# A new list order for every engine, from a planner that prices dependent neighbours on ScalarE and VectorE

## The chip, the cores and the metric

The kernel runs on one core of one Trainium2 chip. The metric is the device time of one execution in microseconds (us). Each run has a state: fast, or slow when it is over 1.5% above the fastest run of the same kernel. Fast runs are compared with fast runs. All inputs are drawn anew from one fixed seed, and every kernel's output is compared with the reference.

## The reference

```python
# x: 8 batches x 8 heads x 512 tokens x 64; state: 8 x 8 x 32 x 64, both fp32
scores = scale * x @ state.T;   a  = softmax(scores);   xread = a  @ state
scores2 = scale * state @ x.T;  a2 = softmax(scores2);  sread = a2 @ x
attn = concatenate([xread, sread], axis=2)          # 544 rows a batch
x = attn.transpose(0, 2, 1, 3).reshape(8 * 544, 512)
h = x @ w_in                                        # w_in  512 x 2048
r = maximum(h, 0)
g = s * (r * r) + b                                 # s, b: scalars
out = g @ w_out                                     # w_out 2048 x 512, fp32 out
```

## The kernel before

The kernel never forms `xread`. For each batch it multiplies the state by `w_in` (blocks `M`, after `Mps`), and a hidden tile `h` is the attention weights `a` times `M`. ScalarE applies the relu, VectorE squares it into `g`. The product with `w_out` (tiles `wo`, four quarters) is plain for batch 0 and uses one Strassen level for the rest, with operand sums `pd` (of `g`) and `u` (of `wo`) made by VectorE. The bias `b` times the column sums of `w_out` (`wsum`) is added at the end, so `wsum` needs all four `wo` quarters.

`E` holds exponentiated scores. `aT` is `E` transposed by a DMA; only `V`, the state's own read, computes with it (and a gate, shown below, holds the load of batch 3's x until batch 1's `aT` has landed). `xT` is the transposed x of batches from 2 on, needed by `T`, their scores. `wo` quarter 3 (`wo3`) is the last weight to arrive.

What runs on the chip is a set of fixed lists, one per engine. They are made when the program is built, by a list scheduler with durations and priorities.

```python
class Plan:
    def order(self, filler, fill_until, ready):
        def settle(i):                  # when may operation i start?
            own = set(ops[i][0])
            since[i] = max(
                [ops[i][8]]             # "after": never planned earlier than this
                + [ready[n] + (0.0 if own == {made_on.get(n)} else self.hop) for n in ops[i][3]]
            )
# ... each free engine takes the ready operation of lowest priority number ...
                end = done = now + dur
                if land is not None:
                    kind, span = land
                    if kind == "load":
                        done = max(channel, end + 2.0) + span     # fixed here, once
                        channel = max(channel, done)
# ...
                    elif kind == "tp" and e == "SP" and now < channel + 4.0:
                        done = end + max(span, min(8.0, 6.0 - 0.75 * (now - channel)))
                        channel = max(channel, now + 2.0) + 1.1
# ...
    SEQ = "wi0 wi1 wi2 wo0 wo1 wi3 wo2 x2 wo3 x1 x0 x3"      # the loads' order on GpSimd's queue
# ... loads: nc.gpsimd.dma_start, fp32 in memory to fp16 on chip
            if b == 3:                                        # x of batch 3 waits for aT of batch 1
                nc.gpsimd.tensor_copy(gate, A[1]["aT"][:, :, 0, 0])
# ... the transposes of E, on SyncE's queue
            nc.sync.dma_start_transpose(a["aT"][:, g], a["E"][g])
            add(
                ("SP", 1.2), kD + 5, aT_dma(b, g), [("E", b, g)] + [("q", b)] * 0,
                [("aT", b, g)], [Eb, ("aT", f"aT{b}")], ("tp", K["la"] if b < 2 else K["lb"]), after=K["a2"] + 2 * g,
            )
# ... at the end the lists are emitted in order of planned time
    for step in sorted(plan.order(filler, 14.0, landed), key=lambda t: t[:2]):
        step[3](step[2])
```

`channel` is the time until which the planner takes the DMA engines as busy, and `after=K["a2"]` the earliest planned time of the `aT` transposes.

The softmax here doesn't subtract the row's maximum and nothing guards it: scores larger than these inputs give would overflow.

Of the kernel before, what the change touches and what calls it, by code (L numbers as in the profile page):

```python
# [13 lines left out]
class Plan:  # L14


    def __init__(self, caps, hop=0.2, look=0.4, solo=0.0, late=0.0):
        self.caps, self.hop, self.look, self.solo, self.late = caps, hop, look, solo, late
        self.ops, self.pool_of, self.users = [], {}, {}

    def add(self, eng, key, fn, needs=(), makes=(), bufs=(), land=None, tiled=False, after=0.0, spare=0.0):
# [6 lines left out]
    def order(self, filler, fill_until, ready):  # L28
        ready = dict(ready)
        ops = self.ops  # L30
        waits, count, cand = {}, {}, {e: set() for e in ("PE", "ACT", "DVE", "POOL", "SP")}
        since, made_on = {}, {}

        def settle(i):
            own = set(ops[i][0])
            since[i] = max(
                [ops[i][8]]
                + [ready[n] + (0.0 if own == {made_on.get(n)} else self.hop) for n in ops[i][3]]
            )
            for e in ops[i][0]:  # L40
                cand[e].add(i)

        for i, o in enumerate(ops):
            open_ = [n for n in set(o[3]) if n not in ready]
            count[i] = len(open_)
            for n in open_:
                waits.setdefault(n, []).append(i)
            if not open_:
                settle(i)
# [25 lines left out]
        while done_n < len(ops) and now < getattr(self, "horizon", 1e9):  # L75
            for e in free_at:
# [9 lines left out]
                look = self.look if e in ("ACT", "DVE") else 0.06  # L86
# [26 lines left out]
                i = best[1]  # L113
# [28 lines left out]
                for m in makes:  # L142
                    for j in waits.pop(m, ()):
                        count[j] -= 1
                        if count[j] == 0:
                            settle(j)
# [15 lines left out]
def kernel(  # L162
# [17 lines left out]
    B, H, S, D = x.shape  # L180
# [29 lines left out]
    def att_ps(shape, dtype, name):  # L210
        return psA.tile(shape, dtype, tag="att", name=name)

    def mm(out, lhsT, rhs, start=True, stop=True, tp=None, is_transpose=None):
        return nc.tensor.matmul(  # L214
            out,
            lhsT,
            rhs,
            start=start,
            stop=stop,
            tile_position=tp,  # L220
            is_transpose=is_transpose,
            skip_group_check=True,
        )
# [22 lines left out]
    def xf_part(b, i):  # L246
        return xf[2 * b + i // 2][:, 2 * (i % 2) : 2 * (i % 2) + 2]
# [9 lines left out]
    for i in range(4):  # L257
# [15 lines left out]
    ident32 = konst.tile([P, P], FP32, name="ident32")  # L273

    K = dict(
        h1=16.1, hs=1.0, M0=-6.0, M1=4.5, T1=13.8, x2=17.3, T2=21.6, D2=23.7, M2=46.3, V0=38.1, V1=37.9, u=27.3,
        us=-13.3, pd1=13.7, o0=25.7, o2=34.4, w=23.8, r=4.7, T=-9.2, D=10.2, Mb=5.5, V=-3.3, S=3.3, S0=-1.1,
        E=-3.5, L=-5.8, E0=-4.8, L0=0.4, E1=-10.7, L1=-2.6, a4=-9.1, Mc=10.1, pd=19.7, solo=18.2, f0=6.0,
        f1=17.4, mc=-12.4, hsr=-8.2, Ssr=2.8, jE00=17.6, jE01=14.7, jL00=5.7, jL01=21.9, jR00=5.9, jR01=-2.7,
        jE10=2.7, jE11=-4.4, jL10=-8.1, jL11=-22.4, jR10=-2.0, jR11=-2.5, jM0=-1.9, jM1=6.2, xc=1.5, a2=38.2,  # L280
        lx=9.7, la=8.1, lb=11.1, rs=29.4, xs=-1.4, x1=10.8, rL=1.3, a4L=-14.8, McL=5.6, mcL=1.9, soloL=8.6,
    )
    A = {b: {"E": {}, "a4": {}} for b in range(B)}
    G, PD, U, SN, OSB = {}, {}, {}, {}, {}
# [18 lines left out]
    def copy_on(e, dst, src):  # L303
# [11 lines left out]
        solo=K["solo"], late=K["soloL"],  # L315
# [55 lines left out]

    gate = konst.tile([P, 2], FP16, name="gate")
    nc.gpsimd.tensor_copy(gate, xf_part(0, 2)[:, 0, 0:2])
    SEQ = "wi0 wi1 wi2 wo0 wo1 wi3 wo2 x2 wo3 x1 x0 x3"
    seq = [(t[:-1], int(t[-1])) for t in SEQ.split()]
    for n, it in enumerate(seq):
        key = -40 + n
# [40 lines left out]
    for k in range(16):  # L418
        b, i = 4 + k // 4, k % 4
# [108 lines left out]
    def E_exp(b, g):  # L528
        def fn(e):
            a = A[b]  # L530
            if "rs" not in a:
                a["rs"] = apool.tile([P, NG, 2], FP32, name=f"rs_{b}", tag="rs", bufs=3)
            a["E"][g] = apool.tile([P, S], FP16, name=f"E_{b}_{g}", tag=f"E{g}", bufs=4)
            for m in range(2):
                kw = {} if b < 2 else dict(accum_out=a["rs"][:, g, m : m + 1])
                nc.scalar.activation(  # L536
                    a["E"][g][:, 256 * m : 256 * m + 256], a["T"][m][:, g, :], AF.Exp, scale=scale, **kw
                )
# [5 lines left out]
    def E_sum(b, g):  # L544
        def fn(e):
            nc.scalar.activation(junk, A[b]["E"][g], AF.Copy, accum_out=A[b]["rs"][:, g, 0:1])

        return fn

    def D_mm(b, g):  # L550
        def fn(e):
            A[b][f"D{g}"] = att_ps([P, S], FP32, f"D_{b}_{g}")
            mm(A[b][f"D{g}"], bones16, A[b]["E"][g])

# [16 lines left out]
    def a4_mul(b, g):  # L571
        def fn(e):
            A[b]["a4"][g] = apool.tile([P, S], FP16, name=f"a4_{b}_{g}", tag=f"a4{g}")
            ENG[e].tensor_mul(A[b]["a4"][g], A[b]["E"][g], A[b][f"R{g}"])

# [85 lines left out]
    for b in range(B):  # L661
# [71 lines left out]
        for g in range(2):  # L733
            Eb, Rb, a4b = (f"E{g}", f"E{b}{g}"), (f"R{g}", f"R{b}{g}"), (f"a4{g}", f"a4{b}{g}")
            Dps = ("att", f"D{b}{g}")
            rs = ("rs", f"rs{b}")
# [363 lines left out]
    for b in [*range(1, B), "sr"]:  # L1100
        nb = B if b == "sr" else b
        for n in range(7):
            bank, xa, xw, first, last = STEPS[n]
            own = [("att", f"osr{bank}")] if b == "sr" else []
# [70 lines left out]
```

## Time and profile before

| | before |
|---|---|
| median of the first 3 runs | 209.92 us (209.05 to 346.59) |
| profiled run | 209.67 us, fast, clock 1.00 |
| TensorE busy | 97% of the span |
| wait on `wo3` ends (GpSimd) | 33.73 us |
| column sums `wsum` start | 35.14 us |
| `T` of batch 2 starts | 47.45 us |
| first `V` starts | 54.59 us |

The run of 346.59 us is a single outlier and enters no comparison.

The timelines of TensorE, VectorE and GpSimd have four marks. The columns are start (us), duration, engine, source line, operation, out<-in, sizes and count, and in brackets the idle time just before and what ended it:

```profile
35.14 1.05 PE L214 MATMUL wsum_ps<-wo,ones 128*32 128x512 f16 x16
47.45 0.43 PE L214 MATMUL T<-xT,stT 64*32 64x256 f16 x16
54.59 0.42 PE L214 MATMUL V<-xn,aT 128*32 128x64 f16 x32
...
34.28 0.42 DVE L892 TENSOR_TENSOR u<-wo 128x512 f16<-128x512 f16 x1
...
33.73 0.18 POOL L406 CAST stf<-wo 128x2 f32<-128x2 f16 x1 [4.77 <-DMA wo<-in_moe_w_out_dram]
```

The GpSimd line is a small copy that starts as soon as `wo3` has landed, so it is a clock for that transfer. There is no DMA among the four parts of the chain. Two pieces of the chain itself, in order of time (start, duration, what):

```profile
35.82 1.14 DVE g L813 x2
...
49.57 0.61 DVE M L307
```

### The profile page before, as it was taken

How to read it: one execution, taken by the hardware profiler on the slowest of the kernel's cores; microseconds unless marked ns; L12 is line 12 of the kernel's file. 1: busy time of each engine (PE TensorE's matmuls, PEld its weight loads, DVE VectorE, ACT ScalarE, POOL GpSimd, SP SyncE). 2: the span in 40 equal slices, each digit the busy share in tenths (PEclk: the TensorE clock that was granted, in tenths of full speed). 3: DMA queues.
4: the chain of work that ended last, by engine and by line, in shares of the span. 5: the costliest groups of instructions: out<-in, count | busy, mean ns of one | idle time of the engine just before them, and what ended most of it. 6: DMA issues, size and time to landing. Idle time of an engine off the chain costs nothing.

```text
span 207.9 us, 4900 instructions
## 1 busy us (share of the span) xinstructions
PE 201.5 (97%) x1956; PEld 133.5 (64%) x1956; DVE 172.0 (83%) x340; ACT 131.2 (63%) x291; POOL 42.4 (20%) x67
## 2 busy tenths in 40 slices
PE   7998999998999999999999999999999999999993
PEld 3832444444767777666667766776677667888882
DVE  3588997999889686799999999999997999787652
ACT  2489998715675467878865877478756884465000
POOL 0853000132512131411602150411021101200000
PEclk9999999999999999999999999999999999999999
DMA  6999999997998529757972474363013502111132
GB/s 192 303 205 203 206 211 199 143 246 155 162 210 102 140 75 171 123 129 105 145 120 95 110 119 92 79 154 83 0 50 111 102 3 57 54 50 52 52 128 76
DMA packets 44423, 26.05 MB, mean 125 GB/s; under 512 B 26480, under 2 KB 42608, under 8 KB 44400
## 3 DMA queue, kind: packets, MB, share of 16 engines
q0 software_dynamic: 14976, 15.73, 39.8%
q1 hardware_dynamic: 29136, 9.84, 25.9%
q8 instruction: 15, 0.25, 0.5%
q10 hardware_dynamic: 288, 0.16, 0.3%
q14 instruction: 8, 0.07, 0.1%
HBM read 19.43 MB, written 8.91 MB: 136 GB/s over the span
## 4 chain that ended last, share of the span: by engine, by line
PE 86%; DVE 8%; ACT 4%; issue 1%
PE o L214 45%; PE h L214 23%; PE h_sr L214 3%; PE osr L214 3%; PE Mps L214 3%; PE warm_ps L214 3%; PE xTps L214 2%; DVE g L813 2%; PE D L214 2%; ACT g L806 1%; PE V L214 1%; DVE pd L829 1%; DVE osb L966 1%; PE T L214 1%; DVE pd L838 1%; DVE pd L840 1%
## 5 line engine op out<-in xcount | busy, mean ns | idle before, releaser
L806 ACT ACTIVATE g<-h 128x512 f16<-128x512 f32 x127 | 73.0, 598 | 32.1 <-PE h L214 30.7
L214 PE MATMUL h<-a,M 128*128 128x512 f16 x256 | 71.9, 379 | 1.0 <-ACT g L806 0.7
L214 PEld LDWEIGHTS <-pd 128*128 128x128 f16 x448 | 43.0, 98 | 20.1 <-issue 0.4
L214 PEld LDWEIGHTS <-g 128*128 128x128 f16 x400 | 38.6, 98 | 18.6 <-issue 2.3
L214 PE MATMUL o<-wo,g 128*128 128x256 f16 (+1 forms) x288 | 47.5, 296 | 0.3 <-DVE osb L966 0.3
L214 PE MATMUL o<-u,pd 128*128 128x256 f16 x336 | 46.8, 273 | 0.0
L813 DVE TENSOR_TENSOR g<-g 128x1024 f16<-128x1024 f16 x64 | 44.2, 699 | 2.1 <-ACT g L806 1.6
L1074 POOL DMA_DIRECT2D out_dram<-c x24 | 16.3, 681 | 100.7 <-DVE c L1062 100.7
L214 PEld LDWEIGHTS <-M 128*128 128x128 f16 x256 | 24.7, 98 | 14.5 <-issue 3.3
L1062 DVE SCALAR_TENSOR_TENSOR c<-o,sb_cols,bias_bc 128x512 f32<-128x512 f32 x28 | 21.0, 750 | 10.1 <-PE o L214 9.5
L307 DVE CAST M<-Mps 128x512 f16<-128x512 f32 x33 | 21.7, 681 | 0.5 <-PE Mps L214 0.5
L305 ACT CAST M<-Mps 128x512 f16<-128x512 f32 x31 | 17.6, 594 | 3.5 <-PE Mps L214 3.5
L829 DVE TENSOR_TENSOR pd<-g 128x1024 f16<-128x1024 f16 x28 | 19.2, 685 | 0.2
L1062 DVE SCALAR_TENSOR_TENSOR c<-o,sb_cols,c 128x512 f32<-128x512 f32 x21 | 15.7, 748 | 4.0 <-PE o L214 3.4
L214 PE MATMUL o<-u,g 128*128 128x256 f16 x112 | 17.8, 273 | 0.0
L365 POOL DMA_DIRECT2D xn<-in_x_dram x20 | 15.7, 832 | 4.3 <-DMA wi<-in_moe_w_in_dram 4.0
L214 PE MATMUL o<-wo,pd 128*128 128x256 f16 x112 | 16.5, 273 | 0.0
L536 ACT ACTIVATE E<-T 128x256 f16<-128x256 f32 x24 | 8.9, 384 | 10.6 <-PE T L214 10.6
L840 DVE TENSOR_TENSOR pd<-g,pd 128x512 f16<-128x512 f16 x28 | 11.8, 421 | 0.5
L838 DVE TENSOR_TENSOR pd<-g,pd 128x512 f16<-128x512 f16 x28 | 11.7, 419 | 0.3
L560 ACT ACTIVATE L<-D 128x512 f32<-128x512 f32 x16 | 9.5, 594 | 1.6 <-PE D L214 1.3
L567 ACT ACTIVATE R<-L 128x512 f16<-128x512 f32 x16 | 10.1, 630 | 0.5
(81 smaller groups left out, 156.5 us busy)
## 6 DMA issues: line engine op xcount, KB each, us to landing
out_dram<-c POOLq DMA_DIRECT2D x24, 256.0 KB, 2.7
xf<-in_x_dram SPq DMA_DIRECT2D x8, 256.0 KB, 5.3
wi<-in_moe_w_in_dram POOLq DMA_DIRECT2D x4, 512.0 KB, 9.6
wo<-in_moe_w_out_dram POOLq DMA_DIRECT2D x4, 512.0 KB, 16.0
xn<-in_x_dram POOLq DMA_DIRECT2D x4, 512.0 KB, 21.2
xn<-in_x_dram POOLq DMA_DIRECT2D x16, 128.0 KB, 3.9
out_dram<-osb POOLq DMA_DIRECT2D x4, 256.0 KB, 4.8
out_dram<-c SPq DMA_DIRECT2D x4, 256.0 KB, 2.5
```

Source lines behind the costliest of these rows:

```text
L214: return nc.tensor.matmul(out, lhsT, rhs, start=start, stop=stop, tile_position=tp, is_transpose=is_transpose, skip_group_check=True,)
L305: nc.scalar.copy(dst, src)
L307: ENG[e].tensor_copy(dst, src)
L365: nc.gpsimd.dma_start(out=xn[b][:, h0:h1].rearrange("p h c d -> p h (c d)"), in_=x[b, h0:h1].rearrange("h (q c) d -> q h (c d)", q=P),)
L567: nc.scalar.activation(A[b][f"R{g}"], A[b][f"L{g}"], AF.Exp, scale=-1.0)
L806: nc.scalar.activation(g_of(name, f), OSB["h", name, f], AF.Relu)
L813: ENG[e].tensor_mul(g, g, g)
L829: nc.vector.tensor_tensor(pd[:, :, 0:2], g4[:, :, 1:2, :].to_broadcast((P, 2, 2, t)), g4[:, :, 0:4:3, :], ALU.subtract,)
L838: nc.vector.tensor_tensor(pd[:, :, 2], g4[:, :, 3], pd[:, :, 0], ALU.subtract)
L840: nc.vector.tensor_tensor(pd[:, :, 3], g4[:, :, 2], pd[:, :, 2], ALU.subtract)
L1062: nc.vector.scalar_tensor_tensor(t, src, s_bc, add, ALU.mult, ALU.add)
L1074: ENG[e].dma_start(dst[:, rows:SCH:2, hD * h : hD * h + hD], SN[b, name])
```

## The change

The intent: where an instruction needs the result of its direct predecessor on ScalarE or VectorE, it starts about 0.1 us later than an independent one would (the prediction below has the lines: 0.12 us on VectorE). The planner now counts that, so it tends to put something else between the two; all priorities were searched again under the new rule, and one pair of loads was exchanged.

```diff
-    def __init__(self, caps, hop=0.2, look=0.4, solo=0.0, late=0.0):
+    def __init__(self, caps, hop=0.2, look=0.4, same=0.1, solo=0.0, late=0.0):
@@ settle
-                + [ready[n] + (0.0 if own == {made_on.get(n)} else self.hop) for n in ops[i][3]]
+                + [ready[n] + ((self.same if own <= {"ACT", "DVE"} else 0.0) if own == {made_on.get(n)} else self.hop) for n in ops[i][3]]
@@ K = dict(...), most of its numbers; cut to one
-        ... xc=1.5, a2=38.2,
+        ... xc=4.3, a2=26.1,
@@
-    SEQ = "wi0 wi1 wi2 wo0 wo1 wi3 wo2 x2 wo3 x1 x0 x3"
+    SEQ = "wi0 wi1 wi2 wo0 wi3 wo1 wo2 x2 wo3 x1 x0 x3"
```

In the lists that come out, the Ln/Exp pairs that are direct neighbours on ScalarE go from 16 to 14, dependent neighbours on VectorE from 54 to 37 (counted in the finished lists, by the plan's own dependences). On SyncE four `aT` transposes move ahead of the `xT` transposes (`a2` is their earliest planned time), and on GpSimd the load of batch 3's x moves ahead of the first output stores.

More of the change, by code (lines that the diff above doesn't have):

```diff
@@ L14 @@
 class Plan:
-    def __init__(self, caps, hop=0.2, look=0.4, solo=0.0, late=0.0):
-        self.caps, self.hop, self.look, self.solo, self.late = caps, hop, look, solo, late
+    def __init__(self, caps, hop=0.2, look=0.4, same=0.1, solo=0.0, late=0.0):
+        self.caps, self.hop, self.look, self.solo, self.late, self.same = caps, hop, look, solo, late, same
         self.ops, self.pool_of, self.users = [], {}, {}
@@ L275 @@
     K = dict(
-        h1=16.1, hs=1.0, M0=-6.0, M1=4.5, T1=13.8, x2=17.3, T2=21.6, D2=23.7, M2=46.3, V0=38.1, V1=37.9, u=27.3,
-        us=-13.3, pd1=13.7, o0=25.7, o2=34.4, w=23.8, r=4.7, T=-9.2, D=10.2, Mb=5.5, V=-3.3, S=3.3, S0=-1.1,
-        E=-3.5, L=-5.8, E0=-4.8, L0=0.4, E1=-10.7, L1=-2.6, a4=-9.1, Mc=10.1, pd=19.7, solo=18.2, f0=6.0,
-        f1=17.4, mc=-12.4, hsr=-8.2, Ssr=2.8, jE00=17.6, jE01=14.7, jL00=5.7, jL01=21.9, jR00=5.9, jR01=-2.7,
-        jE10=2.7, jE11=-4.4, jL10=-8.1, jL11=-22.4, jR10=-2.0, jR11=-2.5, jM0=-1.9, jM1=6.2, xc=1.5, a2=38.2,
-        lx=9.7, la=8.1, lb=11.1, rs=29.4, xs=-1.4, x1=10.8, rL=1.3, a4L=-14.8, McL=5.6, mcL=1.9, soloL=8.6,
+        h1=19.5, hs=-3.4, M0=-3.4, M1=15.0, T1=18.0, x2=17.7, T2=21.0, D2=33.0, M2=48.2, V0=33.6, V1=36.6,
+        u=33.8, us=-12.0, pd1=10.1, o0=26.7, o2=37.8, w=23.8, r=-4.2, T=-7.4, D=10.2, Mb=5.5, V=-1.1, S=3.3,
+        S0=-1.1, E=1.7, L=-5.8, E0=0.6, L0=2.3, E1=-1.3, L1=-1.6, a4=-12.6, Mc=1.1, pd=19.5, solo=12.4, f0=-3.1,
+        f1=16.8, mc=-6.0, hsr=-4.2, Ssr=1.8, jE00=7.8, jE01=15.1, jL00=5.7, jL01=22.2, jR00=11.5, jR01=-3.7,
+        jE10=-0.4, jE11=0.0, jL10=-14.1, jL11=-5.0, jR10=-3.9, jR11=1.2, jM0=-1.5, jM1=3.1, xc=4.3, a2=26.1,
+        lx=10.0, la=7.2, lb=10.2, rs=37.2, xs=-6.8, x1=18.0, rL=1.3, a4L=-14.8, McL=1.3, mcL=1.8, soloL=8.6,
     )
```

## The prediction

> **What bounds the kernel now.** I read in this order: the page (busy shares), the table of stretches, the chain of waits, then the timelines of the engines from 5 to 60 us and of the transfer queues.
>
> From the page and from the table of stretches (columns: stretch, length, busy us and instructions of TensorE, weight loads, VectorE, ScalarE, GpSimd, then granted clock, DMA share, GB/s):
>
> ```profile
> PE 201.5 (97%) x1956; PEld 133.5 (64%) x1956; DVE 172.0 (83%) x340; ACT 131.2 (63%) x291; POOL 42.4 (20%) x67
> ...
> 10.00:15.00 5.00, 4.86 (x54) 2.15 (x52) 4.25 (x8) 4.28 (x12) 2.99 (x4) 1.00 1.24 205
> 15.00:20.00 5.00, 4.14 (x37) 1.52 (x38) 4.05 (x8) 4.93 (x11) 1.76 (x2) 1.00 1.24 204
> 45.00:50.00 5.00, 4.66 (x50) 1.83 (x48) 4.86 (x9) 1.57 (x8) 0.45 (x2) 1.00 0.75 144
> 50.00:55.00 5.00, 4.78 (x81) 3.55 (x82) 4.17 (x9) 3.42 (x7) 1.98 (x4) 1.00 1.14 168
> 60.00:80.00 20.00, 20.00 (x257) 14.80 (x256) 16.95 (x33) 11.62 (x27) 4.88 (x7) 1.00 0.72 127
> ```
>
> TensorE bounds the kernel. From 55 us to the end of the matmuls it is never idle, and the M blocks of successive batches start at 93.75, 115.26 and 136.73: 21.5 us a batch. The work of a batch gives the same: 16 hidden tiles x 0.43 = 6.9, 112 Strassen matmuls x 0.109 = 12.2, four M blocks 1.7, D, T and V 0.9: 21.7. That stage has no slack, so another list order can give nothing there. What can be won lies before 55 us.
>
> The chain of waits, in order of time (start, us, what), shows where the chain leaves TensorE:
>
> ```profile
> 12.92 0.47 PE o L214 x16
> 13.39 1.20 ACT E L536 x4
> 14.91 0.66 ACT L L560
> 15.60 0.63 ACT R L567
> 16.23 0.98 ACT g L806 x2
> ...
> 20.81 0.51 ACT g L806
> 21.36 1.08 PE h L214 x4
> 22.44 0.86 PE o L214 x4
> ```
>
> From 13.4 to 21.3 us ScalarE is the bound (4.93 of 5 us busy), while TensorE waits or runs warm-up matmuls. From 11.46 to 21.36 (9.9 us) the TensorE timeline holds one T (0.23), 48 M matmuls (2.1), 8 hidden tiles (8 x 0.43 = 3.45) and two D (0.44): 6.2 us. So 3.7 us are lost, with 8 warm-ups filling part. From 21.36 to 47.45 its steps follow back to back. A second loss, 0.5 us at 49.1 and 0.2 us at 50.2, comes from VectorE, as the timeline says:
>
> ```profile
> 49.62 0.38 PE L214 MATMUL o<-wo,g 128*128 128x256 f16 x2 [0.34 <-DVE osb L966]
> 50.22 0.39 PE L214 MATMUL D<-E,bones 128*128 128x512 f16 x1 [0.22 <-DVE M L307]
> ```
>
> All that better ordering could win is thus 3.7 + 0.7 = 4.4 us, 2.1%, if every gap closed.
>
> **What the Trainium skill says.** "VectorE: DVE Perf Modes", section "The DRAIN you can't avoid": the next VectorE op does not start before the pipe is empty, and a semaphore costs nothing extra. This trace disagrees for a needed neighbour:
>
> ```profile
> 42.22 0.68 DVE L829 TENSOR_TENSOR pd<-g 128x1024 f16<-128x1024 f16 x1
> 42.94 0.42 DVE L838 TENSOR_TENSOR pd<-g,pd 128x512 f16<-128x512 f16 x1
> 43.40 0.42 DVE L840 TENSOR_TENSOR pd<-g,pd 128x512 f16<-128x512 f16 x1
> 43.74 2.12 DVE L813 TENSOR_TENSOR g<-g 128x1024 f16<-128x1024 f16 x2
> ```
>
> L829 to its dependent L838 takes 0.72 from start to start; L829 to an op that does not need it takes 0.60 (37.55 to 38.15). L838 to L840 takes 0.46, L840 to a stranger 0.34. So a dependent neighbour costs 0.12 us. ScalarE shows about the same: Ln to its Exp 0.63, Exp to the next 0.54.
>
> "DMA: Bandwidth & Descriptors", section "Queues, rings and completion order": each DMA engine takes turns between its queues, packet by packet. Here that fits: around 36 to 40 us, where transposes run beside loads, the rate falls to 114 and 186 GB/s in 2 us stretches, from about 200 before.
>
> **The change part by part.** The planner now adds 0.1 us between dependent neighbours on ScalarE and VectorE, with new priorities, and the fourth quarter of the first weights (wi3) is loaded before the second quarter of the output weights (wo1). No instruction disappears. The planner does not run on the chip; only the lists differ, which I compared by engine.
>
> Dependency pairs: in the stage that ScalarE bounds, two Ln/Exp pairs are pulled apart: 2 x 0.1 = 0.2 us. On VectorE before 50 us four or five pairs of u and pd: 5 x 0.12 = 0.6 us, partly hidden.
>
> Walking the first stage with the old durations: the old list has ScalarE do four exponentials of batch 1 (13.38 to 14.59) before its M cast, so the second hidden matmul waits until 15.12. The new list casts one half on ScalarE at 13.54 and the other on VectorE beside it; hidden tiles 0 and 1 start near 14.25 and the first relu at 15.08 instead of 16.14. But TensorE then has M blocks of the second quarter ahead of tiles 2 and 3, which wait for wi1 (landed near 15.6), so part of the 0.9 us is given back. Going on with relus at 0.49, casts at 0.47 and Ln or Exp at 0.54: tiles 4 and 5 at 17.35, tiles 8 and 9 from 20.5, the first output block at 21.7. At 22.6 the new list has done 10 tiles and 1 output block; the old one had at 23.14. That is 0.55 us ahead, and it is still 0.55 at 28.6 (18 tiles, 8 M blocks and 3 output blocks, against 17, 7 and 3 at 28.33). Later three hidden tiles in a row (6, 7, 8 of batch 1) meet two hidden buffers: 0.3 us lost. At the turn to batch 1's outputs VectorE now does the third eviction (osb) ahead of two of the pd ops, 0.46 + 0.34 = 0.8 us earlier: up to 0.5 of the 0.7 us there is saved. Sum: 0.55 - 0.3 + 0.5, with the VectorE pairs 0.1 to 0.2: about 0.9 us faster.
>
> Against it stands something that the labels of the change don't say. In the transfer list of SyncE the four transposes of the batch 0 and 1 weights (aT<-E) move ahead of the xT transposes, and the next x load moves ahead of the first output stores. The old list:
>
> ```profile
> 23.25 0.34 SPq L410 DMA_DIRECT2D stf<-in_state_dram x1
> 28.98 0.69 SPq L396 DMA_DIRECT2D sb_in<-in_moe_s_dram x1
> 29.73 0.55 SPq L397 DMA_DIRECT2D sb_in<-in_moe_b_dram x1
> 31.31 3.93 SPq L445 DMA_TRANSPOSE xT<-xn x3
> 35.34 0.54 SPq L407 DMA_DIRECT2D stf<-in_state_dram x1
> 35.93 5.14 SPq L445 DMA_TRANSPOSE xT<-xn x1
> 41.17 5.55 SPq L615 DMA_TRANSPOSE aT<-E x4
> ```
>
> SyncE's first entry waits for wo1, which now comes sixth, so 25.8 instead of 23.05 us. Three aT transposes then issue from 26.4 to 30.1 and reach the engines some 3.7 us later (packets of the first xT transposes show only at 35.0), just when the x of batch 2 and the last output weights (wo3) come in. The packets of the loads next to transposes moved about 125 KB per us against 205 alone, for rows of 512 bytes; wo3 has rows of 1024 bytes, so by turns I estimate 160. Batch 2's x: 308 KB left at 30.1, / 125 = 2.5, so 32.6. wo3: 524 / 160 = 3.3, so 35.9, against 33.73 (the end of the GpSimd wait on it). TensorE needs wo3 for the column sums near 34.5 and VectorE for u near 34.4. That is 1.4 us of wait in both, or 2.5 if a pause of a microsecond as around 37 us comes with it. VectorE takes part of it back, having less left by then; following it to osb number 3 (48.83 in the old trace) I get 49.2 to 50.4. So this part costs 1.5 to 2.5 us against the gain of 0.9. T of batch 2 (47.45) also needs all xT transposes; four more 128 KB transposes before them bring its slack of about 2 us to near zero, up to 1 us more.
>
> **The rivals.** (1) Order alone counts, loads are on time: 209.92 - 0.9 = 209.0. For it: the old lists had wo3 1.4 us ahead of its use (33.73, 35.14). (2) The early transposes delay wo3 and xT: 210.7 to 211.7. For it: the falling rates above; against it: the byte sum up to 47 us is unchanged except for the early x load. (3) The stage before 21 us closes nearly wholly, because many casts move to better places: 206 to 207. Against it: ScalarE's work there is unchanged and wi1, wi2 and wo0 land no earlier. (4) Nothing moves, because VectorE is 93 to 97% busy from 20 to 50 us and sets the turn: 209.9.
>
> **Range and chances.** (1) and (2) get about equal weight, (3) a little, which gives 209.6 us. The range from 207.6 to 212.6 holds (1), most of (2) and part of (3). Faster by over 2% means under 205.7, nearly the whole 4.4 us: 0.03. Slower by over 2% means over 214.1, both delays in full and more: 0.05. Within 2%: 0.92.
>
> **What would show it.** First relu of batch 0 near 15.1 (old 16.14) and first output block near 21.7 (old 22.27) prove the walk. A wait of TensorE's column sums or VectorE's L892 ended by the wo transfer, near 34 to 37 us, proves (2); no such wait proves (1). T of batch 2 later than 48 with a wait on xT shows the second delay. The batches after 60 us must keep 21.5 us. It would be wrong if that period changed, or if a wait I didn't walk (PSUM buffers of M against D) stops TensorE before 30 us.

## More of the kernel before

The page's part 4 says where the chain that ended last lay, as shares of the span:

```profile
PE 86%; DVE 8%; ACT 4%; issue 1%
```

Neither `wsum` nor `u` nor `T` has a bracket: none of them waits.

## The result, and the profile after

| | before | after |
|---|---|---|
| median, same chip | 209.54 us (6 runs) | 212.54 us (6 runs, 211.63 to 217.02) |
| ratio of fast runs | 1 | 1.013, 95% interval 1.0091 to 1.0169 |
| mean of the fast runs | 209.48 us (5) | 212.21 us (6, one of them not among those of the median) |

A ratio is the mean time of one kernel's fast runs over that of the other's in the same rounds, so it is not quite the ratio of the medians or means quoted here. The time is within 2%, and 3.0 us above the predicted point by the medians. It lies only 0.06 us inside the predicted range (207.6 to 212.6), and the median includes a slow run; the mean of the fast ones lies 0.4 us inside.

The profiled execution of the kernel after fell in the slow state (217.02 us, mean clock 0.984). Its order of events can be read, but its sizes are those of a slow run; the fast profiles of the experiments below give the sizes.

First the page, busy shares and chain. TensorE has 3.1 us more of busy time and two points less of share, and DMA, absent from the chain before, is now its second part (in this slow run):

```profile
PE 204.6 (95%) x1957; PEld 135.2 (63%) x1957; DVE 170.1 (79%) x338; ACT 132.3 (61%) x293; POOL 43.1 (20%) x67
...
PE 85%; DMA 5%; ACT 4%; SPq 3%; DVE 0%; issue 0%
```

The first stage went as walked. The timelines of ScalarE and of TensorE show the first relu (two in a row) and the first output block:

```profile
15.06 1.13 ACT L806 ACTIVATE g<-h 128x512 f16<-128x512 f32 x2
...
21.44 1.02 PE L214 MATMUL o<-wo,g 128*128 128x512 f16 x4
```

15.06 against 15.08 predicted and 16.14 before; 21.44 against 21.7 predicted and 22.27 before. The new order is ahead until then. What follows is a different picture, on TensorE, VectorE and GpSimd:

```profile
34.26 0.83 PE L214 MATMUL wsum_ps<-wo,ones 128*32 128x512 f16 x12
38.33 0.62 PE L214 MATMUL wsum_ps<-wo,ones 128*32 128x512 f16 x4 [3.24 <-DMA wo<-in_moe_w_out_dram]
...
54.21 0.28 PE L214 MATMUL T<-xT,stT 64*32 64x256 f16 x2 [2.29 <-DMA xT<-xn]
...
62.05 0.42 PE L214 MATMUL V<-xn,aT 128*32 128x64 f16 x32
...
38.31 0.42 DVE L892 TENSOR_TENSOR u<-wo 128x512 f16<-128x512 f16 x1 [4.47 <-DMA wo<-in_moe_w_out_dram]
...
38.34 0.44 POOL L406 CAST stf<-wo 128x2 f32<-128x2 f16 x1 [8.82 <-DMA wo<-in_moe_w_out_dram]
```

The column sums do twelve of their sixteen matmuls and then stand 3.24 us for `wo3`, which lands 4.6 us later than before (38.34 against 33.73). `u` on VectorE waits for the same transfer. A second wait, 2.29 us, comes at `T` of batch 2, for `xT`. The first `V` is 7.46 us later than before, and the whole run 7.35 us (217.02 against 209.67 for the two profiled runs): the loss is complete by then.

The chain of this run, which is a slow one, goes through the second of these transfers, `xT`, and not through `wo3`:

```profile
35.40 2.00 SPq L445
...
42.84 11.32 DMA xT<-xn
```

The cause suspected in the prediction can be read from SyncE's queue (its instructions only issue a transfer, so their durations are not those of the transfers):

```profile
26.52 5.02 SPq L615 DMA_TRANSPOSE aT<-E  x3
...
33.02 2.19 SPq L615 DMA_TRANSPOSE aT<-E  x1
35.40 6.77 SPq L445 DMA_TRANSPOSE xT<-xn  x3
...
42.84 3.98 SPq L445 DMA_TRANSPOSE xT<-xn  x1
```

Three `aT` transposes go out from 26.52 to 31.5, while x of batch 2 and `wo3` come in; the first `xT` is issued at 35.40 where it was 31.31. The stretches (columns as in the prediction) show what TensorE lost there:

```profile
35.00:40.00 5.00, 1.76 (x13) 0.58 (x9) 1.66 (x6) 1.08 (x3) 0.44 (x1) 0.77 1.27 150
...
50.00:55.00 5.00, 2.71 (x40) 0.95 (x37) 3.33 (x7) 0.38 (x3) 1.44 (x2) 0.98 1.20 260
55.00:60.00 5.00, 5.00 (x29) 3.06 (x28) 2.82 (x7) 2.84 (x12) 0.54 (x1) 0.68 0.40 89
```

In 35 to 40 us TensorE, VectorE and ScalarE all stand, so it is a common wait. Then the clock: 0.77, and 0.68 after the second wait. Summing (1 - clock) times length over the four stretches where it fell (0.77, 0.89 in 40 to 45, 0.98, 0.68) gives 1.15 + 0.55 + 0.10 + 1.60 = 3.4 us, part of which lies in the waits themselves. That is an estimate, from these four clocks, of what the lower clock can explain at most, of the 4.8 us between this run and the mean of the fast ones (212.21). The cost of the change that is explained below is that of the fast runs, 2.2 to 2.7 us.

From 60 us on nothing has changed: the same M blocks stand at 101.44 and 122.91 us, 21.5 us apart as before.

### The profile page after: what moved, and what is told of

Read it like the earlier page. It is cut to its first block, busy times and chain, and to the rows that moved or that the text cites. A ratio compares the mean times of both kernels' runs of the same rounds, so it can differ in the third digit from the quotient of the medians.

```text
span 215.2 us, 4903 instructions
## 1 busy us (share of the span) xinstructions
PE 204.6 (95%) x1957; PEld 135.2 (63%) x1957; DVE 170.1 (79%) x338; ACT 132.3 (61%) x293; POOL 43.1 (20%) x67
## 4 chain that ended last, share of the span: by engine, by line
PE 85%; DMA 5%; ACT 4%; SPq 3%; DVE 0%; issue 0%
PE o L214 44%; PE h L214 23%; DMA xT<-xn 5%; PE Mps L214 3%; PE h_sr L214 3%; SPq L445 3%; PE osr L214 3%; PE warm_ps L214 3%; PE xTps L214 2%; ACT g L806 2%; PE D L214 2%; PE V L214 1%; PE T L214 1%; ACT M L305 1%; ACT E L536 0%
## 5 line engine op out<-in xcount | busy, mean ns | idle before, releaser
L214 PE MATMUL h<-a,M 128*128 128x512 f16 x256 | 72.7, 383 | 0.4 <-ACT g L806 0.3
L214 PEld LDWEIGHTS <-g 128*128 128x128 f16 x400 | 39.2, 99 | 18.5 <-issue 4.9
L214 PE MATMUL o<-wo,g 128*128 128x256 f16 (+1 forms) x288 | 48.0, 302 | 0.0
L214 PE MATMUL o<-u,pd 128*128 128x256 f16 x336 | 47.9, 273 | 0.0
L813 DVE TENSOR_TENSOR g<-g 128x1024 f16<-128x1024 f16 x64 | 43.1, 684 | 2.4 <-ACT g L806 2.2
L305 ACT CAST M<-Mps 128x512 f16<-128x512 f32 x33 | 18.6, 591 | 10.3 <-PE Mps L214 10.2
L307 DVE CAST M<-Mps 128x512 f16<-128x512 f32 x31 | 20.5, 682 | 3.1 <-PE Mps L214 3.1
L214 PE MATMUL o<-u,g 128*128 128x256 f16 x112 | 17.3, 273 | 0.0
L214 PE MATMUL o<-wo,pd 128*128 128x256 f16 x112 | 16.0, 273 | 0.0
```

The lines of the kernel that those rows point to most:

```text
L214: return nc.tensor.matmul(out, lhsT, rhs, start=start, stop=stop, tile_position=tp, is_transpose=is_transpose, skip_group_check=True,)
L305: nc.scalar.copy(dst, src)
L307: ENG[e].tensor_copy(dst, src)
L813: ENG[e].tensor_mul(g, g, g)
```

## The experiments

All were run with five rounds beside the kernel before. The first four shared one chip and eleven runs of before (mean 209.29 us), the next four another (209.59), the last four a third (209.39). Where a list is edited, the edit takes the finished list of the plan and moves entries, with `put_after(x, y)` for "take x out and put it directly behind y". Waits between instructions follow from the order of the list, so such an edit keeps the data right as long as no reader is put ahead of its writer.

**The kernel after again, unchanged.**

> The changed kernel as it is, to get its profile in the undisturbed state. Theory A (early transposes slow the loads): ratio to before 1.010 to 1.017; TensorE again waits 3 us for the column sums near 34 to 38 us (wo transfer) and some 2 us in T of batch 2 (xT transfer), now at a granted clock of 1.0. Rival B (the stalls belong to the slow state alone): these waits shrink below 1 us at full clock, and the extra 3 us are spread over the batches after 60 us.

Two runs were fast (mean 211.51 us, ratio 1.0105, 1.0085 to 1.0126) and two slow (215.8). So on this chip the fast cost is 2.2 us. The profile fell in the slow state again. TensorE's timeline:

```profile
37.13 0.62 PE L214 MATMUL wsum_ps<-wo,ones 128*32 128x512 f16 x4 [1.74 <-DMA wo<-in_moe_w_out_dram]
...
52.98 0.28 PE L214 MATMUL T<-xT,stT 64*32 64x256 f16 x2 [1.84 <-DMA xT<-xn]
```

Both waits are there again, shorter: 1.74 and 1.84 us. Rival B, that the stalls belong to the slow state, is therefore not settled by this run; the fast profiles below settle it for `wo3`, not for `T`.

**The transfers put back, all compute lists as after.** Batch 3's x load again follows the fourth output store, and the four `aT` follow `xT`.

```diff
+    x3 = steps.pop(at(("x", 3, 0)))
+    steps.insert(put_of(("read", 0, 3)) + 1, x3)          # behind the 4th output store
+    last = ("xT4", 2, 3)
+    for b, g in ((0, 0), (1, 0), (0, 1), (1, 1)):
+        put_after(("aT", b, g), last)
+        last = ("aT", b, g)
```

> The changed kernel with only the SyncE entries aT of batches 0 and 1 moved back behind the xT transposes of batch 2, and the load of x of batch 3 back behind the fourth output store; all three compute lists stay as changed. Theory A: both TensorE waits go, the last output weights land near 33.7 us, ratio to before 0.992 to 0.998 (0.9 us faster, 208.6 to 209.0). Rival C (the new compute lists or the swapped weight loads cost the time): ratio stays at 1.008 or more, with other waits in their place.

Measured: median 208.53 us, mean 208.72, 0.57 us below before (ratio 0.997, 0.9948 to 0.9992), all six runs fast. Against the mean of the fast unchanged runs the gain is 2.8 us. TensorE's timeline has no wait left at these places, while `u` on VectorE still waits 0.63 us:

```profile
34.77 1.05 PE L214 MATMUL wsum_ps<-wo,ones 128*32 128x512 f16 x16
47.45 0.44 PE L214 MATMUL T<-xT,stT 64*32 64x256 f16 x14
...
53.99 0.42 PE L214 MATMUL V<-xn,aT 128*32 128x64 f16 x32
...
34.98 0.43 DVE L892 TENSOR_TENSOR u<-wo 128x512 f16<-128x512 f16 x1 [0.63 <-DMA wo<-in_moe_w_out_dram]
```

The expected landing of `wo3`, near 33.7 us, was missed: GpSimd's wait for it ends at 35.01. So the new compute order, with its exchanged loads, is worth about half a microsecond, and the moved transfers cost 2.8. Where the half microsecond is gained is also visible: `T` stands exactly where it stood before (47.45), and from `T` to `V` it now takes 6.54 us against 7.14. The lead of the first stage is gone by `T` (VectorE has waited the 0.63 us at `u` on the way); the turn to batch 1's outputs is what is kept.

**The kernel before with the four `aT` moved early, nothing else.**

```diff
+    last = ("stf", 1)
+    for b, g in ((0, 0), (1, 0), (0, 1)):
+        put_after(("aT", b, g), last)
+        last = ("aT", b, g)
+    put_after(("aT", 1, 1), "sb")
```

> The kernel before with only the four aT transposes moved early in the SyncE list, to where the changed kernel has them (load of x of batch 3 stays late). Theory A: wo3 lands 2 to 4 us later, the column sums wait for it, ratio to before 1.008 to 1.016. Rival C: within 0.3% of before, as the compute lists are the old ones.

Measured: median 212.32 us, mean 3.1 us above before (ratio 1.0147, 1.0127 to 1.0168), all four runs fast. This is nearly the mirror image of the run above; the three transposes go out 2.1 us earlier than in the kernel after (24.41 against 26.52). SyncE's queue:

```profile
24.41 4.02 SPq L615 DMA_TRANSPOSE aT<-E  x3
```

And TensorE's, VectorE's and GpSimd's timelines:

```profile
38.14 0.40 PE L214 MATMUL wsum_ps<-wo,ones 128*32 128x512 f16 x4 [2.06 <-DMA wo<-in_moe_w_out_dram]
50.78 0.61 PE L214 MATMUL T<-xT,stT 64*32 64x256 f16 x14
...
57.95 0.42 PE L214 MATMUL V<-xn,aT 128*32 128x64 f16 x32
...
38.12 0.42 DVE L892 TENSOR_TENSOR u<-wo 128x512 f16<-128x512 f16 x1 [3.65 <-DMA wo<-in_moe_w_out_dram]
...
38.15 0.44 POOL L406 CAST stf<-wo 128x2 f32<-128x2 f16 x1 [8.46 <-DMA wo<-in_moe_w_out_dram]
```

Four transfers moved, in an otherwise old kernel, bring `wo3` 4.4 us later, and everything behind it 3.3 to 3.4 us later (`T` 50.78 against 47.45, `V` 57.95 against 54.59). There is no wait at `T`. This profile is a fast one at full clock, so the wait for `wo3` does not need the slow state.

**The kernel after with only batch 3's x load put back.**

```diff
+    x3 = steps.pop(at(("x", 3, 0)))
+    steps.insert(put_of(("read", 0, 3)) + 1, x3)
```

> The changed kernel with only the load of x of batch 3 put back behind the fourth output store; transposes stay early. Theory A: the wait for wo3 (3 us) stays, since this load comes later than that; the wait in T of batch 2 gets shorter by 0 to 2 us; ratio to before 1.006 to 1.013. If T keeps its wait of 2.3 us whole, the early x load has no share and the transposes alone explain both waits.

Measured: median 211.72 us, mean 211.66, ratio 1.0112 (1.0096 to 1.0128); the unchanged kernel's fast runs had 211.51. All four runs were fast. The timelines of TensorE and VectorE:

```profile
35.72 0.40 PE L214 MATMUL wsum_ps<-wo,ones 128*32 128x512 f16 x4 [0.78 <-DMA wo<-in_moe_w_out_dram]
49.43 0.43 PE L214 MATMUL T<-xT,stT 64*32 64x256 f16 x16
...
40.64 0.20 DVE L391 COPY sb_rows<-sb_in 128x64 f32<-128x64 f32 x1 [1.45 <-DMA sb_in<-in_moe_b_dram]
```

The wait at `T` is gone. Whether it came from the early x load or belongs to the slow state is not shown, since both profiles that have it are slow ones and no profile of a fast run of the unchanged kernel exists. The time of fast runs did not fall: the early x load costs them nothing that can be measured. The wait for `wo3` is only 0.78 us here. A tiny load that comes behind three of the transposes in SyncE's list (`sb_in`, the scalars s and b) now holds VectorE 1.45 us, and the chain that ended last goes through it, and not through `wo3`:

```profile
31.59 8.94 DMA sb_in<-in_moe_b_dram
```

This run and the one with all transfers put back differ in the place of the four `aT` alone. By their means (211.66 and 208.72 us) these four transposes cost 2.9 us, with the compute lists and the x load the same. Of that VectorE loses 0.72 us at `u` (35.70 against 34.98) and 1.45 at `sb_in`, 2.2 together; the two profiled runs differ by 2.35.

**The kernel before with two `aT` early.**

```diff
+    put_after(("aT", 0, 0), ("stf", 1))
+    put_after(("aT", 1, 0), ("aT", 0, 0))
```

> The kernel before with two of the four aT transposes early (the first of batch 0 and of batch 1), the other two after the xT transposes. Theory A as a dose: with none early 209.25, with four 212.3, so about 1.5 us slower here, ratio 1.005 to 1.010, with a shorter wait of the column sums for wo (0.5 to 1.5 us instead of 2.1). Rival D (a threshold: only the whole queue stalls): within 0.2% of before or as slow as with four.

Measured: median 211.81 us, mean 2.26 us above before (ratio 1.0109, 1.0069 to 1.0149), a little more than expected. The profiled run was the fastest of the six (210.83 us, 1.16 above the profiled run of before). The timelines of GpSimd and TensorE, and two pieces of the chain:

```profile
35.73 0.44 POOL L406 CAST stf<-wo 128x2 f32<-128x2 f16 x1 [6.85 <-DMA wo<-in_moe_w_out_dram]
...
35.06 1.06 PE L214 MATMUL wsum_ps<-wo,ones 128*32 128x512 f16 x16
...
12.14 23.54 DMA wo<-in_moe_w_out_dram
...
35.70 0.44 DVE u L892
```

The expected wait of the column sums (0.5 to 1.5 us) did not come: TensorE does not wait for `wo3` here. VectorE does, at `u`, which starts 1.42 us later than before (35.70 against 34.28), and the chain goes from `wo3` through `u`. So the loss does not need a wait of TensorE's column sums; the wait of `u`, the other one that the prediction named, is enough.

The landing of `wo3` follows the dose: none early 33.73, two 35.73, four 38.15 us, about 1 us for each transpose of 128 KB (single profiles).

**The kernel before with four plain copies of the same tiles at that place.** The copies go to tiles nobody reads (one is the tile of the warm-ups, which are over by then) and are added to the four `aT`, which stay late.

```diff
+            nc.sync.dma_start(OSB["dup"][i % 3], A[b]["E"][g])    # 3 behind stf, 1 behind sb
```

> The kernel before with four added plain copies of 128 KB (the same exponentials, rows of 1024 bytes, to buffers that nobody reads) where the changed kernel has its early transposes; the transposes stay late. If the bytes alone take the time of the weights, 4 x 128 KB at some 200 KB per us delay wo3 by up to 2.6 us and the time rises by 2 us or more (ratio 1.009 to 1.015, as with the transposes). If it is the transposes' small packets and taking turns with them, wo3 comes at most 1.5 us later than 33.7 and the ratio is 1.000 to 1.005.

Measured: median 210.71 us, mean 1.31 us above before (ratio 1.0064, 1.0029 to 1.0099). SyncE's queue and GpSimd's timeline:

```profile
23.92 1.17 SPq L1166 DMA_DIRECT2D dup<-E  x2
...
35.62 0.44 POOL L406 CAST stf<-wo 128x2 f32<-128x2 f16 x1 [6.11 <-DMA wo<-in_moe_w_out_dram]
```

This lies between the two expectations. The same bytes without the transposition delay `wo3` by 1.9 us, with it by 4.4; the cost in time is 1.3 against 3.1 us. So bytes alone are under half of it, by single profiles for `wo3` and by runs on two chips for the time. The first two plain copies issue in 1.17 us together, three transposes in 4.02; whether the rest is the size of the pieces, or a share of the engines that a transpose holds, these runs don't tell.

**One eviction moved at the turn of the kernel before.** The prediction had given 0.5 us to the third eviction (`osb`) going ahead of two `pd` sums.

```diff
+    put_after(("read", 0, 2), ("pd", 1, 3, 0))
```

> The kernel before with one entry of VectorE's list moved: the third eviction of batch 0's output (osb) goes ahead of two of the three last pd ops, as the changed list has it. By the prediction's walk the wait of 0.34 us at 49.3 goes and up to 0.5 us is saved: ratio 0.9975 to 0.9990. If the turn was not bound by this eviction: 0.9995 to 1.0005.

The edit was faulty: in the emitted order the eviction came ahead of the last quarter of its own sum, and TensorE then waited for the eviction, in its timeline:

```profile
48.73 1.02 PE L214 MATMUL o<-wo,g 128*128 128x512 f16 x4 [2.04 <-DVE osb L966]
```

Its 210.93 us (ratio 1.0088) say nothing about the turn. The output also passed the comparison with a quarter of one block's sum missing, so that comparison is no proof of such an edit.

**The mended edit.** The eviction comes right behind the last part of its sum, the two `pd` behind it.

```diff
+    put_after(("read", 0, 2), ("o", 0, 2, 3))
+    put_after(("pd", 1, 3, 1), ("read", 0, 2))
+    put_after(("pd", 1, 3, 2), ("pd", 1, 3, 1))
```

> The edit of e7 mended: the third eviction of batch 0's output goes ahead of two pd ops in VectorE's list and stays behind the matmuls whose sum it reads (in e7 it stood ahead of the last quarter of that sum, so that kernel gave a wrong block and its time says nothing). By the prediction's walk the wait near 49.3 goes and up to 0.5 us is saved: ratio 0.9975 to 0.9990 against before. If the turn was not bound by this eviction: 0.9995 to 1.0005.

Measured: median 209.36 us, ratio 1.0000 (0.9979 to 1.0021). TensorE's timeline:

```profile
49.62 0.39 PE L214 MATMUL D<-E,bones 128*128 128x512 f16 x1 [0.47 <-DVE M L307]
```

The wait for the eviction is gone, and the one behind it, for an M cast that VectorE now does later, has grown from 0.22 to 0.47 us. From `T` to `V` it takes 6.89 us against 7.14. The moved eviction alone brings 0.25 of the 0.5 us in this profile and nothing measurable in the time; the interval would still allow 0.4.

**The transfers put back and the old load order too.**

```diff
+    # as in the second experiment, and:
+    swap(("wo", 1), ("wi", 3))
```

> The changed kernel with its transfers late (as in e2) and also the old order of the weight loads (wo1 before wi3). The new compute lists want wi3 near 25 us; it would land near 25.9, so TensorE waits some 0.5 to 1 us in the M block of the last quarter and the ratio goes from 0.997 (e2) to 0.999 to 1.003. If it stays at 0.997 the swap of the loads is worth nothing.

Measured: median 209.06 us, ratio 0.9995 (0.9954 to 1.0037). The expected wait for the first weights appears in TensorE's timeline:

```profile
25.27 0.62 PE L214 MATMUL Mps<-wi,stT 64*32 64x512 f16 x16 [0.87 <-DMA wi<-in_moe_w_in_dram]
```

Whether the exchange pays is not settled: 0.9995 and 0.997 have intervals that overlap widely, and worked out from both the old load order could be from 0.5 us faster to 1.5 us slower. In this profile `wo3` lands at 33.45 us, `u` does not wait, and the first `V` comes 0.37 us earlier than with the new load order (53.62 against 53.99), in spite of the wait for the first weights.

**The kernel after with one number of the plan put back.**

```diff
-        ... a2=26.1,
+        ... a2=38.2,
```

> The changed kernel with one number of the planner put back, the earliest time of the aT transposes (26.1 to 38.2, a2), so that the planner itself moves them and the x load late. Theory A: as fast as e2, ratio 0.994 to 0.999; a one-number repair. If the replanned lists bring other waits: 1.000 or more.

Measured: median 208.78 us, mean 0.46 below before (ratio 0.9977, 0.9953 to 1.0000). The planner made all lists anew, and again there is no wait for `wo3` or `xT`. So a single number, the earliest planned time of the `aT`, turns a loss of 2.2 to 2.7 us into a gain of 0.5, whose interval reaches zero.

**The same with the new rule set to zero.**

```diff
-    def __init__(self, caps, hop=0.2, look=0.4, same=0.1, solo=0.0, late=0.0):
+    def __init__(self, caps, hop=0.2, look=0.4, same=0.0, solo=0.0, late=0.0):
-        ... a2=26.1,
+        ... a2=38.2,
```

> As e10, with the new rule of the planner switched off (0.0 instead of 0.1 us between dependent neighbours), new priorities kept. If keeping dependents apart is worth what its label says, this is slower than e10 by 0.3 us or more (ratio to e10 1.0015 and up; the rule takes 0.12 us from about five pairs before 50 us). If the rule only reshuffles: within 0.1% of e10 either way.

Measured: median 209.58 us (ratio to before 1.0018, 0.9993 to 1.0043), mean 209.75 against 208.93 with the rule: 0.8 us slower, as the first of the two expectations had it.

**The kernel before with the rule alone**, its priorities and load order as they were.

```diff
-                + [ready[n] + (0.0 if own == {made_on.get(n)} else self.hop) for n in ops[i][3]]
+                + [ready[n] + ((0.1 if own <= {"ACT", "DVE"} else 0.0) if own == {made_on.get(n)} else self.hop) for n in ops[i][3]]
```

> The kernel before with the new rule alone (0.1 us between dependents on ScalarE and VectorE), old priorities and load order; its list keeps the transposes late. If the rule itself is the gain: ratio 0.995 to 0.999. If the priorities belong to the rule and were searched with it, the order of batches 2 to 4 falls apart (their exponentials now stand ahead of batch 3's relus) and it is slower, ratio 1.005 to 1.02.

Measured: median 212.77 us, mean 3.4 above before (ratio 1.0162, 1.0139 to 1.0186). The loss lies elsewhere: `wo3` lands at 33.47 us and `T` starts at 45.28, 2.2 us earlier than before. The table of stretches has a hole of 2.6 us in a stage that had none before (20.00 of 20 us busy), and TensorE's timeline shows its waits, none of which is put down to a transfer (one of 0.89 us has no releaser in the profile). Here is one for an M cast that stands late on VectorE:

```profile
60.00:80.00 20.00, 17.38 (x266) 11.57 (x264) 13.13 (x23) 10.00 (x24) 4.21 (x6) 1.00 0.90 130
...
71.52 0.82 PE L214 MATMUL h<-a,M 128*128 128x512 f16 x3 [0.67 <-DVE M L307]
```

Taken together, the last two say that rule and priorities belong together: priorities that were searched with the rule lose 0.8 us without it, and priorities that were searched without it lose 3.4 us with it. What the rule is worth by itself, after a search of its own for each side, stays open.

### The loss is over at the first V

The profiled runs, each with the landing of `wo3` (end of GpSimd's wait), the start of the first `V` and the time of the same run, as differences from before (33.73, 54.59, 209.67):

| kernel | `wo3` | first `V` | run |
|---|---|---|---|
| after, slow | +4.6 | +7.5 | +7.4 |
| after again, slow | +3.4 | +6.3 | +6.2 |
| after, x load late | +2.0 | +1.8 | +1.7 |
| after, all transfers late | +1.3 | -0.6 | -0.7 |
| after, `a2` back | +0.4 | -0.7 | -0.5 |
| before, four `aT` early | +4.4 | +3.4 | +3.4 |
| before, two `aT` early | +2.0 | +1.2 | +1.2 |
| before, four plain copies | +1.9 | +1.0 | +1.3 |

The last two columns agree within 0.3 us in every row, so each of these changes acts before the first `V` and is simply carried to the end. The first column orders the rows only roughly, for two reasons. In the kernel after with all transfers late `wo3` is 1.3 us late and costs VectorE only 0.63 us. And `wo3` is not always the transfer that the chain goes through: it is in the kernel before with two or four `aT` early and with the plain copies, but it is `sb_in` in the kernel after with the x load late, and `xT` in the two slow profiles of after. In the kernel before the loss follows VectorE: `u` starts 1.31, 1.42 and 3.84 us later than before (plain copies, two, four early), and the profiled runs are 1.29, 1.16 and 3.38 us longer.

## Why the prediction was right or wrong

**The bound, and where a gain can lie: right for the late batches, incomplete for the turn.** After 60 us no kernel with the new priorities changed its pace, and every loss or gain in the table above was complete by the first `V`. That an order can lose there is shown by the rule alone (2.6 us between 60 and 80). "TensorE bounds the kernel" needs an addition: the chain of before runs over VectorE from 35.82 to 50.2 us. The prediction did follow VectorE to the third eviction when it put a size on the delay, and that was the right engine. Its figure for VectorE, 93 to 97% busy from 20 to 50 us, is misread too: the table has 3.85 of 5 us (77%) from 30 to 35 and 4.93 (99%) from 40 to 45.

**The walk of the first stage: right, and what became of it too hopeful.** First relu and first output block came within 0.02 and 0.3 us of the walk, and the wait for a hidden buffer, put at 0.3 us, came with 0.25. The sum "0.55 - 0.3 + 0.5, with the VectorE pairs 0.1 to 0.2: about 0.9 us" is too large: with the transfers out of the way the order brings 0.5 to 0.6 us. By `T` the lead is used up in that profile (47.45 in both kernels), after a wait of 0.63 us for `wo3` on VectorE; with `a2` put back, where `u` does not wait, `T` stands at 47.21. What is left is the term for the turn: 0.5 predicted, 0.6 found between `T` and `V` (6.54 against 7.14 us). The reason given for that term was too narrow, since the eviction moved alone gave 0.25 there and no measurable time.

**The early transposes: right in the cause, too small in size, and one path missing.** The prediction read from the list of transfers that `aT` would go ahead of `xT` and delay `wo3`, and that waits of the column sums and of `u`, ended by the `wo` transfer, would prove it. They came. The landing of `wo3`, worked out from rates as 35.9, or about 37 with a pause, was 35.73 in the one fast profile of the new lists with early transposes (x load late), 38.34 and 37.15 in the slow ones of after, and 38.15 in the old kernel, where the transposes go out earlier. So this term is not what made the cost too small in that fast profile. What the walk doesn't have is the wait for `sb_in`: the prediction shows its two lines in SyncE's list, but follows `wo3` and `xT` only. It held VectorE 1.45 us in the fast profile and 1.13 in the second slow one. What "VectorE takes back" was 0.5 of 3.84 us, with four early in the old kernel. The cost, put at 1.5 to 2.5 us, measured 2.9 (the four `aT` alone, new lists) and 3.1 (the same, old lists). The prediction calls the fall to 114 and 186 GB/s fitting for queues that take turns. That fall does not show the turns, since the rate is that of all queues together, and no run here shows them.

**The x load and T: right as an event, open in its cause, without an effect in the fast runs.** The wait at `T` came (2.29 and 1.84 us, both in slow profiles) and was gone with the x load put back, in a fast one; the fast runs cost the same with and without it.

**The weights of the rivals: about half of why the point was 3 us low.** Rival (1), that loads stay on time, was given the same weight as rival (2). The argument for it was 1.4 us of slack of `wo3`. That slack was known, and the estimate for the delay (2.2 to 3.3 us, from 33.73 to 35.9 or 37) already exceeded it, so (1) should have had little weight. The other argument against (2), that the sum of bytes up to 47 us does not change, fails in that the transfers' order decides who waits, and in that four transposes cost their neighbours more than their bytes. But the middle of rival (2), 211.2, is only 1.6 us above the point; most of the rest is the gain and the cost that were mis-sized. Its range has a slip as well: 209.92 - 0.9 + 1.5 to 2.5 is 210.5 to 211.5, not 210.7 to 211.7. That the result still lies in the stated range, by 0.06 us, is luck.

**Why the plan did not see it** is read from its code rather than shown by a run: the landing of a load is fixed when it is issued, and transposes planned afterwards never push it back. Putting `a2` back by hand, which the search had moved freely, is what repaired the time.

## What to carry to other kernels

When a schedule is searched against a model, look for what the model leaves out, and read the transfer lists as carefully as the compute lists: here half a microsecond won by order was lost five times over by four small transfers moved forward. In this kernel transfers without urgency belonged behind the last load that someone waited for, although their queue stood idle. And when a transfer is moved, follow every transfer behind it to its first reader, the tiny ones too, on the engine that the chain runs over at that time: here the delay went through `wo3`, `sb_in` or `xT`, depending on the run. And where a slack has been read (1.4 us) and a delay estimated above it, the wait is the likely outcome, not one of two equal ones. The best kernels are the two repaired ones, 208.53 and 208.78 us, by their ratios 0.3 and 0.2% below the kernel before (the interval of the second reaches 1.0000).

## What the Trainium skill lacked or had wrong

- "Advanced Engine Details and Errata", section "X-Bar Transpose (TRN2)", says that "TRN2 transpose DMAs are as fast as regular DMAs". Beside other loads they cost more here: four transposes of 128 KB bring the last weights 4.4 us later and the kernel 3.1 us, four plain copies of the same tiles 1.9 and 1.3 us. From issue to landing the early transposes took 9.8 us in the median, the copies 6.2 to 6.4. No page gives the cost to neighbouring loads.
- "TensorE: Matmul & The Clock Gate", section "Part 1: The HAM clock gate (the "warmup" mystery)", gives half rate after an idle window of about 3.4 us. Here the granted clock fell to 0.50 after waits of 3.24 us and of 1.74 us, in slow profiles only, while in the fast profile of the old kernel with early transposes a wait of 2.06 us left it at 1.00. So neither the length alone nor 3.4 us decides. The lines of the stretches, of the kernel after, of the same again and of that old kernel:

```profile
36.00:38.00 2.00, 0.00 (x0) 0.00 (x0) 0.00 (x0) 0.00 (x0) 0.00 (x0) 0.92 1.51 160
38.00:40.00 2.00, 1.67 (x9) 0.58 (x9) 1.66 (x6) 0.64 (x2) 0.44 (x1) 0.50 1.37 178
```

```profile
38.00:40.00 2.00, 2.00 (x9) 0.93 (x8) 1.89 (x7) 0.98 (x2) 0.00 (x0) 0.50 1.37 184
```

```profile
36.00:38.00 2.00, 0.09 (x4) 0.00 (x0) 0.00 (x0) 0.49 (x2) 0.00 (x0) 1.00 1.58 132
```

  Of eleven runs of the unchanged kernel after, three were slow; of the 60 runs of the other eleven experiments, none. Why it tips in some runs stays open.
- "VectorE: DVE Perf Modes", section "The DRAIN you can't avoid": a dependent neighbour costs 0.12 us more than an independent one in the trace of before (0.72 against 0.60 us, 0.46 against 0.34). The section doesn't have this; it says that a semaphore after each operation costs nothing extra.
- No page has the same cost on ScalarE: an Exp that needs the Ln just before it starts 0.61 to 0.69 us after it (before); a relu and a cast that don't need it start 0.48 and 0.47 us after such an Ln (with the transfers put back, at 16.22 and 75.97 us). The prediction compared the Exp with what follows the Exp, 0.54, which is another pair.
